# A fused lightning attention and gMLP kernel under another written-out order of its 719 steps

## The chip, the cores and the metric

The kernel runs on one core of one Trainium2 chip. The metric is the device time of one execution in microseconds (us), lower is better. Five engines work side by side, each through its own queue in order: TensorE (PE, the matmuls), VectorE (DVE), ScalarE (ACT), GpSimd (POOL), and SyncE (SP), which here only issues transfers (DMA). An engine that has to wait at one step also holds up every step queued behind it.

## The reference, cut to what matters

Decayed linear attention in blocks of 64 rows over 4 batches, 8 heads, 768 rows and head size 64, followed by a gated MLP whose gate mixes rows with a 768 x 768 matrix:

```python
for b in range(nb):                                   # 12 blocks of 64 rows
    intra = einsum('bhic,bhjc->bhij', qb, kb) * Dmask # lam ** (i - j), lower triangle
    intra = einsum('bhij,bhjd->bhid', intra, vb)
    inter = einsum('bhid,bhde->bhie', qb * lam_pow, kv_state)
    out[:, :, sl] = intra + inter
    kv_state = lam_block * kv_state + einsum('bhsd,bhse->bhde', kb * rev_pow, vb)
x = out.transpose(0, 2, 1, 3).reshape(B, S, H * D)
h = maximum(x @ w_in, 0)                              # 512 -> 1024
u, v = h[..., :512], h[..., 512:]
v_n = (v - mean(v)) / sqrt(var(v) + 1e-06)
v_s = einsum('ts,bsd->btd', w_spatial, v_n) + b_spatial[None, :, None]
y = (u * v_s) @ w_out                                 # 512 -> 512
```

## The kernel before

The decays are powers of one factor per head, so the kernel multiplies the rows of k and q by tables of powers once (`lv`, `lqn`, lines 222 to 227) and then works with a 0/1 mask. All matmul operands are bf16. The work is cut into 12 steps of 256 rows, three to a batch: steps 0 to 2 are batch 0, and so on to steps 9 to 11 for batch 3. Once the three steps of a batch have given their normalised `vn`, the row mixing and the output of that batch can be computed.

The order is fully written out. `ORDER` (line 16) is a string of 719 tokens; `tc.manual_schedule()` (line 610) runs through it, and each token calls one function. Its last letter is the engine: T TensorE, D VectorE, A ScalarE, P GpSimd, S SyncE. The tokens of one letter, read in turn, are that engine's queue. Semaphores are put in where a step reads what another wrote, or overwrites a buffer or PSUM bank that is still read; so an order cannot make a wrong result, but it decides who waits. The numbers behind the name are the step or batch, the part, and the PSUM banks.

| tokens | lines | what they do |
|---|---|---|
| LK, LQ, LV n | 196 | load k, q or v of step n, 512 KB, into one of three buffers (n mod 3), from SyncE |
| lam, BR | 200, 289 | load the 8 factors and the bias row, from ScalarE |
| LB, LN, LL, LX | 216 to 227 | spread the factors, logarithm, the tables of powers |
| msk, idn, posk, one, row | 203 to 240 | mask, identity for the transposes, positions, ones |
| FL k | 309 | k filler matmuls on ones, into a bank that is overwritten later |
| KM, QM n.x | 331 | decayed k or q of half x, f32 to bf16, on VectorE or GpSimd |
| VC, VD n | 185, 181, 183 | v to bf16, whole or in halves |
| TK, TQ; EK, EQ | 366 | transposes on TensorE and their copies out of PSUM (steps 0 to 6) |
| DK, DQ | 344, 348 | the same transposes by DMA, from SyncE (steps 7 to 11) |
| SC, MK | 396, 401 | scores of one half, masked into `a_sb` |
| KP, SY, SX, SA | 425 to 440 | state of the step: matmuls, and the copies and sums of it |
| AV, FN, EX | 468, 459, 481, 487 | attention output, a one-element copy that marks its end, the copy to `xT` |
| WH, CW, CX | 253 to 257 | W_in: four loads, four casts of the v half (CW), two of the u half (CX) |
| WQ, WC, WT, EW | 274 to 563 | W_spatial: six loads, casts, transposes, copies |
| WP, WX | 283 to 286 | W_out: one load of 1 MB, two casts |
| PV, EV, BN | 493, 498, 508 | v = x @ W_in and its relu, row statistics |
| RA, RD, RB, VN | 513 to 532 | 1/sqrt of the variance and the normalised rows `vn` |
| PU, EU | 544, 498 | u, transposed, and its relu |
| GP, PW, GM | 566, 570, 576 | bias put into the bank, the row mixing (6 matmuls) added to it, times u |
| PO, PH; EO, EH; ST, SH | 581 to 604 | output, its copy, its store (256 KB) |
| GN | 536 | a one-element copy on GpSimd that waits for a `vn`, and so holds GpSimd back |

W_in's v half and W_out and two of the W_spatial blocks pass through the same f32 buffer `wst[0]`, so those loads wait for the casts of what lay there. k, q and v have three buffers each, the casts and decays (`kc`, `qc`, `vb`) and the transposed operands (`kT`, `qT`) two.

Of the kernel before, what the change touches and what calls it, by code (L numbers as in the profile page):

```python
# [21 lines left out]
TQ.1.0.1.T FL.4.256.4.1.T TK.1.0.0.T TK.1.1.3.T TQ.1.1.5.T KP.0.2.T AV.0.0.6.4.T QM.2.0.P LK.2.S KM.2.1.P KM.2.0.P
LV.1.S WH.0.S WH.1.S LV.2.S LQ.3.S WH.3.S VD.1.1.P CW.2.P EQ.1.0.1.D SX.0.D EQ.1.1.5.A SY.0.2.A EK.1.1.3.A
FN.0.6.4.D EK.1.0.0.D TQ.2.1.5.T AV.0.1.6.4.T SA.0.1.D EQ.2.1.5.D SC.1.0.1.2.T EX.0.0.6.A EX.0.1.4.A FL.2.256.0.1.T
FL.1.256.3.1.T TQ.2.0.0.T SC.1.1.5.6.T TK.2.1.4.T FL.2.256.3.1.T FL.1.256.3.1.T FL.1.256.3.1.T TK.2.0.3.T
MK.1.0.1.2.D MK.1.1.5.6.D EQ.2.0.0.A VD.1.0.A EK.2.1.4.A KP.1.2.T AV.1.0.0.1.T SY.1.2.D SA.1.0.D FN.1.0.1.D
# [5 lines left out]
EV.2.1.6.A WT.0.0.3.T WT.2.0.5.T EW.2.0.5.A PU.2.1.2.T WT.1.0.0.T BN.2.0.D RD.1.D BN.2.1.D VN.1.1.D RD.0.D RB.0.D
EW.0.0.3.A RA.2.A VN.0.0.A CX.0.P PU.2.0.6.T EU.2.0.6.A VN.0.1.A EW.1.0.0.D RD.2.D LK.3.S PU.1.0.5.T PU.0.0.3.T
VN.2.0.D VN.1.0.D VN.2.1.D LK.4.S WQ.3.S EU.1.0.5.D GP.0.2.0.6.D EU.2.1.2.A GP.0.1.0.5.A EU.0.0.3.A GP.0.3.0.2.A
KM.3.0.P WQ.4.S WQ.5.S LV.3.S LQ.4.S LQ.5.S LV.4.S KM.4.0.P QM.4.0.P QM.4.1.P QM.5.0.P QM.5.1.P VC.4.P PW.0.0.0.1.T
KM.4.1.D KM.3.1.D WC.3.D GM.0.0.0.1.D PW.0.1.0.5.T PW.0.2.0.6.T TK.3.2.0.T WC.4.A EQ.3.2.4.A EK.3.2.0.A WC.5.D
GM.0.1.0.5.D GM.0.2.0.6.D WT.2.1.3.T WT.0.1.1.T EW.0.1.1.D WP.S VC.3.D EW.2.1.3.A GP.0.1.1.6.A PW.0.3.0.2.T
WT.1.1.4.T LK.5.S GM.0.3.0.2.D SC.3.1.0.1.T KP.3.5.T SC.3.0.2.3.T MK.3.1.0.1.D EW.1.1.4.A PW.0.1.1.6.T TK.4.2.0.T
MK.3.0.2.3.D GP.0.3.1.1.A GP.0.2.1.2.A SY.3.5.A PW.0.3.1.1.T SA.3.1.D SX.3.D GM.0.1.1.6.D GP.0.0.1.3.A TQ.4.2.4.T
PW.0.2.1.2.T GM.0.2.1.2.D GM.0.3.1.1.D PW.0.0.1.3.T GM.0.0.1.3.D EK.4.2.0.A EQ.4.2.4.A KM.5.0.P KM.5.1.P  # L40
AV.3.0.5.6.T SC.4.0.1.2.T KP.4.0.T FN.3.5.6.A AV.3.1.5.6.T SY.4.0.D SC.4.1.3.4.T EX.3.1.6.A TQ.5.2.0.T WX.0.A WX.1.A
EX.3.0.5.D MK.4.0.1.2.D SA.4.1.D MK.4.1.3.4.D SA.4.0.D LV.5.S PV.3.1.6.T PU.3.1.5.T PO.0.1.1.T PO.0.3.2.T TK.5.2.4.T
PV.3.0.3.T LV.6.S LK.6.S EK.5.2.4.D EO.0.1.1.A EQ.5.2.0.A EV.3.1.6.A EU.3.1.5.A EO.0.3.2.D VC.5.P AV.4.0.6.0.T
KP.5.6.T SC.5.0.1.2.T EV.3.0.3.A FN.4.6.0.D SC.5.1.4.5.T AV.4.1.6.0.T PU.3.0.3.T VC.6.P SA.5.0.D MK.5.1.4.5.D
MK.5.0.1.2.D KM.6.0.P KM.6.1.P LK.7.S LQ.7.S LQ.6.S KM.7.1.P QM.7.0.P QM.6.0.P QM.6.1.P EX.4.1.0.A EX.4.0.6.A
PV.4.1.0.T PV.4.0.4.T AV.5.0.1.5.T BN.3.1.D FN.5.1.5.D KP.6.2.T AV.5.1.1.5.T EV.4.0.4.A PO.0.2.4.T PO.0.0.6.T
EV.4.1.0.A EX.5.1.5.A EX.5.0.1.A BN.3.0.D PV.5.1.0.T PU.5.1.5.T PV.5.0.1.T KM.7.0.P LV.7.S LV.9.S LQ.8.S LQ.9.S
LK.8.S LV.8.S EO.0.2.4.D EU.3.0.3.A BN.4.1.D RA.3.A RD.3.D GP.1.2.0.4.D GP.1.1.0.3.A SY.6.2.A EV.5.1.0.D
GP.1.0.1.0.A SX.6.A EV.5.0.1.A BN.4.0.D BN.5.1.D BN.5.0.D EO.0.0.6.A RA.4.A PU.4.0.2.T PU.4.1.1.T RD.4.D EU.5.1.5.D
RB.3.D EU.4.0.2.A RA.5.A PO.0.5.6.T PU.5.0.5.T GP.1.1.1.2.A EU.4.1.1.A VN.3.1.A EU.5.0.5.A RD.5.D VN.4.1.D VN.5.0.D  # L50
VN.4.0.D VN.5.1.D EO.0.5.6.D VN.3.0.D SA.6.1.D PO.0.4.1.T TK.6.2.5.T TQ.6.2.6.T EO.0.4.1.A PW.1.1.0.3.T PW.1.1.1.2.T
PW.1.2.0.4.T GM.1.1.1.2.D EQ.6.2.6.D GM.1.1.0.3.D PW.1.0.1.0.T GM.1.2.0.4.D GM.1.0.1.0.D GP.1.3.0.1.A QM.7.1.P
KM.8.0.P KM.8.1.P VC.7.P QM.8.1.P GN.2.1.P QM.8.0.P EK.6.2.5.A GP.1.2.1.0.D GP.1.3.1.2.A DQ.7.S DK.7.S PW.1.3.0.1.T
GM.1.3.0.1.D SC.6.0.5.6.T SC.6.1.3.4.T GP.1.0.0.1.A PW.1.2.1.0.T PW.1.0.0.1.T MK.6.1.3.4.D MK.6.0.5.6.D GM.1.2.1.0.D
GM.1.0.0.1.D PW.1.3.1.2.T GM.1.3.1.2.D AV.6.0.6.0.T FN.6.6.0.A KP.7.3.T SY.7.3.D SC.7.1.4.5.T AV.6.1.6.0.T
SC.7.0.1.2.T EX.6.0.6.A PO.1.4.3.T PO.1.5.6.T QM.9.0.D MK.7.1.4.5.D MK.7.0.1.2.D SA.7.1.D SA.7.0.D EX.6.1.0.A
PV.6.1.4.T EV.6.1.4.D PO.1.0.5.T EO.1.5.6.A VC.8.A EO.1.4.3.A AV.7.0.2.6.T DK.8.S DQ.8.S LK.9.S SC.8.0.0.1.T
FN.7.2.6.A KP.8.6.T SC.8.1.3.4.T AV.7.1.2.6.T EO.1.0.5.A EX.7.0.2.A EX.7.1.6.A MK.8.0.0.1.D SA.8.0.D MK.8.1.3.4.D
BN.6.1.D PV.6.0.5.T PO.1.2.2.T VC.9.A KM.9.1.P KM.9.0.P PV.7.1.6.T EV.7.1.6.D PV.7.0.4.T AV.8.0.0.1.T KP.9.3.T
EV.6.0.5.A GP.2.3.1.6.A EV.7.0.4.A FN.8.0.1.D AV.8.1.0.1.T BN.6.0.D BN.7.0.D EX.8.1.1.A EX.8.0.0.A PU.6.0.5.T  # L60
PU.7.1.4.T GP.2.1.0.1.D SY.9.3.D EU.6.0.5.A EO.1.2.2.D BN.7.1.D EU.7.1.4.A RA.6.A PV.8.1.0.T EV.8.1.0.D PV.8.0.2.T
PU.8.1.3.T PU.6.1.4.T PU.7.0.5.T EV.8.0.2.A EU.8.1.3.A GP.2.2.0.2.A EU.6.1.4.A RA.7.A BN.8.1.D RD.6.D BN.8.0.D
SA.9.1.D RB.6.D VN.6.0.D RD.7.D RA.8.A RD.8.D RB.7.D VN.7.1.A GP.2.0.1.0.A EU.7.0.5.A SX.9.A PO.1.1.3.T PU.8.0.4.T
RB.8.D LQ.10.S LK.10.S ST.0.0.S LV.10.S DK.9.S LQ.11.S VN.7.0.D VN.6.1.D VN.8.0.D VN.8.1.D GP.2.3.0.5.A EU.8.0.4.A
KM.10.0.P QM.9.1.P GN.5.0.P QM.10.0.P QM.10.1.P DQ.10.S LK.11.S ST.0.3.S KM.10.1.P PW.2.3.1.6.T GP.2.2.1.4.D
GM.2.3.1.6.D DQ.9.S KM.11.0.P KM.11.1.P QM.11.0.P QM.11.1.P PW.2.1.0.1.T PW.2.0.1.0.T GP.2.1.1.6.D GM.2.1.0.1.D
GM.2.0.1.0.D PW.2.2.1.4.T PW.2.3.0.5.T ST.0.5.S LV.11.S DK.10.S ST.0.4.S GM.2.3.0.5.D GM.2.2.1.4.D VC.10.A
EO.1.1.3.A GP.2.0.0.3.A PW.2.2.0.2.T GM.2.2.0.2.D SC.9.0.0.1.T SC.9.1.4.5.T PW.2.0.0.3.T PO.1.3.2.T MK.9.0.0.1.D
GM.2.0.0.3.D MK.9.1.4.5.D PW.2.1.1.6.T GM.2.1.1.6.D EO.1.3.2.A KP.10.0.T AV.9.0.1.2.T SY.10.0.D FN.9.1.2.A
SC.10.1.3.4.T SC.10.0.5.6.T AV.9.1.1.2.T EX.9.1.2.A PO.2.0.0.T DK.11.S DQ.11.S ST.1.4.S ST.0.1.S ST.0.2.S EX.9.0.1.D  # L70
PV.9.0.2.T EV.9.0.2.A PV.9.1.1.T MK.10.1.3.4.D MK.10.0.5.6.D EV.9.1.1.A BN.9.1.D SA.10.1.D SA.10.0.D BN.9.0.D
PO.2.3.2.T PU.9.1.3.T VC.11.P EU.9.1.3.A EO.2.0.0.A PO.2.4.5.T EO.2.4.5.A SC.11.1.3.4.T KP.11.6.T SC.11.0.0.1.T
PU.9.0.6.T PO.2.5.5.T MK.11.1.3.4.D RA.9.A RD.9.D MK.11.0.0.1.D SA.11.0.D AV.10.0.3.4.T AV.11.0.0.1.T FN.10.3.4.D
RB.9.D FN.11.0.1.D AV.10.1.3.4.T EO.2.5.5.A AV.11.1.0.1.T EX.11.0.0.A EX.10.0.3.A PO.2.2.5.T EX.10.1.4.D PV.10.1.0.T
PU.10.1.3.T EX.11.1.1.D EV.10.1.0.A EU.10.1.3.A VN.9.0.A PV.10.0.4.T GP.3.1.1.1.D EO.2.2.5.D EO.2.3.2.D BN.10.1.D
EV.10.0.4.A PV.11.1.5.T EV.11.1.5.A EU.9.0.6.D PV.11.0.2.T GP.3.0.1.6.A EV.11.0.2.A BN.10.0.D RA.10.A BN.11.1.D
# [567 lines left out]
```

## Time and profile before

| | |
|---|---|
| median of 3 runs | 145.53 us (145.13 to 146.61) |
| the profiled execution | 144.71 us, of which 143.0 us are its span |
| mean granted TensorE clock | 0.972 |
| busy, TensorE / VectorE / ScalarE / GpSimd | 133.8 / 115.3 / 82.8 / 51.9 us |
| TensorE's share of the chain that ended last | 83% |
| moved by DMA | 33.6 MB, mean 235 GB/s |

The span is what the trace covers; the 1.71 us between it and the time lie around it. The slices of the page cut the span into 40 equal parts of 3.575 us; a digit 9 is 90% busy or more, and PEclk is the granted TensorE clock in tenths of full speed. The chain of waits follows the work that ended last back to the start: each of its pieces is one engine's work, and the next begins where that one released it. Where it stays on one engine, that engine was the limit. The filler matmuls count as TensorE's busy time.

### The profile page before, as it was taken

Reading aid. Unit: us, or ns where it says so; the run is one execution under the profiler, and the core shown is the slowest. Engines: PE = TensorE matmul, PEld = TensorE weight load, DVE = VectorE, ACT = ScalarE, POOL = GpSimd, SP = SyncE. Lnnn points to the kernel's source line nnn. Section 1 sums busy time; section 2 is a strip of 40 time slices with the busy share of each in tenths; the row PEclk is TensorE's granted clock in tenths of the full one; section 3 lists DMA queues with packets and bytes.
Section 4 is the critical chain, followed back from the end, with each engine's and each line's share of the span. In section 5 each row is a group of like instructions: output and inputs, shape, how many; then the busy total and the mean of one; then the engine's idle time right before and its main releaser. Section 6 shows DMA issues by size and latency. Waiting matters only on the chain.

```text
span 143.0 us, 4741 instructions
## 1 busy us (share of the span) xinstructions
PE 133.8 (94%) x1999; PEld 87.7 (61%) x2014; DVE 115.3 (81%) x236; ACT 82.8 (58%) x158; POOL 51.9 (36%) x61
## 2 busy tenths in 40 slices
PE   5969999899999899999999999999999999999990
...
DVE  3399798989997769699399988995798889874760
...
PEclk9975899999999999999999999999999999999998
DMA  3999999899999899959904799998994403930284
GB/s 87 347 347 346 386 323 315 294 339 313 337 302 344 259 288 324 285 166 290 293 0 78 49 282 354 180 142 238 276 257 126 177 5 117 406 139 0 78 324 185
DMA packets 54617, 33.60 MB, mean 235 GB/s; under 512 B 11715, under 2 KB 49859, under 8 KB 54596
## 3 DMA queue, kind: packets, MB, share of 16 engines
...
q8 instruction: 15, 0.25, 0.7%
q10 hardware_dynamic: 148, 0.13, 0.3%
...
## 4 chain that ended last, share of the span: by engine, by line
PE 83%; DVE 9%; ACT 3%; issue 2%; DVEq 0%; ACTq 0%
PE ps L570 21%; PE ps L581 14%; PE ps L493 13%; PE ps L544 11%; PE ps L396 5%; PE ps L366 5%; PE ps L309 4%; PE ps L468 4%; PE ps L425 3%; PE ps L459 2%; DVE st L508 2%; DVE qc L331 2%; DVE kc L331 2%; DVE vn L532 1%; DVE win_sb L183 1%
## 5 line engine op out<-in xcount | busy, mean ns | idle before, releaser
L570 PE MATMUL ps<-wt_sb,vn 128*128 128x384 bf16 x192 | 33.7, 326 | 0.5 <-ACT vn L529 0.3
L331 POOL TENSOR_TENSOR kc<-k_in,lv 128x512 bf16<-128x512 f32 x20 | 20.5, 1043 | 30.0 <-PE ps L493 11.5
L401 DVE TENSOR_TENSOR a_sb<-ps,m 128x1024 bf16<-128x1024 f32 x24 | 28.4, 1211 | 0.7 <-PE ps L425 0.6
L570 PEld LDWEIGHTS <-vn 128*128 128x128 bf16 x192 | 18.3, 98 | 12.3 <-ACT vn L529 0.6
L544 PE MATMUL ps<-xT,win_sb 128*128 128x256 bf16 x192 | 23.6, 273 | 0.5 <-DVE win_sb L183 0.5
L331 POOL TENSOR_TENSOR qc<-q_in,lqn 128x512 bf16<-128x512 f32 x18 | 19.3, 1090 | 10.2 <-DMA q_in<-in_q_dram 5.2
L493 PE MATMUL ps<-win_sb,xT 128*128 128x512 bf16 x89 | 22.3, 379 | 0.4
L581 PE MATMUL ps<-wout_sb,gT 128*128 128x512 bf16 x84 | 22.1, 379 | 0.4
L576 DVE TENSOR_TENSOR gT<-ps,uT 128x384 bf16<-128x384 f32 x32 | 16.8, 551 | 7.1 <-PE ps L570 6.7
L544 PEld LDWEIGHTS <-win_sb 128*128 128x128 bf16 x192 | 18.4, 98 | 5.1 <-DVE win_sb L183 0.7
L181 ACT ACTIVATE ps<-bsp 128x384 f32<-128x384 f32 x23 | 11.2, 490 | 10.7 <-DVE gT L576 6.7
L508 DVE BATCH_NORM_STATS2 st<-vh 128x6 f32<-128x512 bf16 x24 | 16.2, 676 | 1.1 <-ACT vh L498 1.1
L181 ACT ACTIVATE o_sb<-ps 128x512 f32<-128x512 f32 (+1 forms) x14 | 8.0, 579 | 15.4 <-PE ps L581 14.6
L493 PEld LDWEIGHTS <-xT 128*128 128x128 bf16 x96 | 8.8, 98 | 9.6 <-ACT xT L181 0.8
L498 ACT ACTIVATE vh<-ps 128x512 bf16<-128x512 f32 x20 | 11.7, 600 | 4.9 <-PE ps L493 3.2
L181 ACT ACTIVATE xT<-ps 128x512 bf16<-128x512 f32 x20 | 11.0, 598 | 5.8 <-PE ps L468 5.7
L581 PEld LDWEIGHTS <-gT 128*128 128x128 bf16 x92 | 8.7, 98 | 8.6
L498 ACT ACTIVATE uT<-ps 128x512 bf16<-128x512 f32 x20 | 11.7, 590 | 2.0 <-PE ps L544 2.0
L468 PE MATMUL ps<-a_sb,vb 64*64 64x128 bf16 x384 | 10.2, 220 | 0.3 <-issue 0.3
L396 PE MATMUL ps<-qT,kT 64*64 64x128 bf16 x384 | 9.7, 226 | 0.0
L309 PE MATMUL ps<-ones 128*128 128x256 bf16 x32 | 7.5, 368 | 1.6 <-DVE ones L305 1.5
L185 POOL CAST vb<-v_in 128x1024 bf16<-128x1024 f32 (+1 forms) x6 | 5.8, 965 | 7.8 <-PE ps L468 7.8
...
## 6 DMA issues: line engine op xcount, KB each, us to landing
...
```

What stands on the lines that cost most here:

```text
L181: nc.scalar.activation(out=o, in_=i, func=AF.Copy)
L331: vec(e).tensor_tensor(out=dst[n % NCA][:, u].rearrange("p u m o d -> p o (u m) d"), in0=src[n % NIN].rearrange("p (o u) m d -> p o u m d" ...
L396: nc.tensor.matmul(out=pa[o][row(c), w, j], lhsT=kT[n % NTR][row(o), u, j, c * Q64:(c + 1) * Q64], rhs=qv(n, o, u, c), start=(w == 0 and j ...
L401: nc.vector.tensor_tensor(out=a_sb[n % NA][:, i].rearrange("p o w j x -> p o w (j x)"), in0=ps[:, b0:b1 + 1:b1 - b0].rearrange("p o (w y) ...
L468: nc.tensor.matmul(out=po[c ^ o][row(w), c, i], lhsT=vb[n % NCA][row(c), 4 * o + u, j, :], rhs=a[row(c), i, o, w, j, :], start=(r == 0 and ...
L493: nc.tensor.matmul(out=bank(b), lhsT=x[:, slot(c, g)], rhs=win_sb[:, g, DH:DFF], start=(g == 0), stop=(g == NCH - 1))
L498: nc.scalar.activation(out=o, in_=i, func=AF.Relu)
L508: nc.vector.bn_stats(out=st6[p2][:, t], in_=vh[p2][:, t])
L544: nc.tensor.matmul(out=pu[:, f2].rearrange("p (c x) -> p c x", c=2), lhsT=win_sb[:, g, f * P:(f + 1) * P], rhs=x[:, slot(0, g):slot(1, g) ...
L570: nc.tensor.matmul(out=bank(b)[:, 0:HW], lhsT=vn[bb % 2][:, s, f * P:(f + 1) * P], rhs=wt_sb[:, s, i * HW:(i + 1) * HW], start=False, stop ...
L576: nc.vector.tensor_tensor(out=gT[bb % 2][:, f, cols], in0=bank(b)[:, 0:HW], in1=uT[bb % 2][:, f, cols], op=ALU.mult)
L581: nc.tensor.matmul(out=bank(b), lhsT=gT[bb % 2][:, f, t * P:(t + 1) * P], rhs=wout_sb[:, f, :], start=(f == 0), stop=(f == NCH - 1))
```

## The change

Only `ORDER` differs: the same 719 functions are called in another order, on partly other engines and with other PSUM banks; no function is changed. TensorE gets the same 213 tokens, 32 filler matmuls among them. VectorE has 214 tokens instead of 211, ScalarE 152 instead of 160, GpSimd 59 instead of 54, SyncE 81 as before. What moves between engines (tokens before and after):

| | ScalarE | VectorE | GpSimd |
|---|---|---|---|
| decays KM | - | 4, 5 | 20, 19 |
| decays QM | - | 6, 3 | 18, 21 |
| W_in casts CW | 3, 0 | 0, 1 | 1, 3 |
| W_in casts CX | 0, 1 | 1, 0 | 1, 1 |
| v casts VC | 4, 4 | 2, 1 | 5, 6 |
| relus EV and EU | 40, 33 | 8, 15 | - |
| bias GP | 23, 20 | 9, 12 | - |
| vn VN | 7, 9 | 17, 15 | - |
| W_out casts WX | 2, 1 | 0, 1 | - |

The loads, in SyncE's order up to step 5:

```
before: LK.0 LQ.0 LQ.1 LK.1 LV.0 LQ.2 LK.2 LV.1 WH.0 WH.1 LV.2 LQ.3 WH.3 WQ.0 WQ.1 WQ.2 WH.2
        LK.3 LK.4 WQ.3 WQ.4 WQ.5 LV.3 LQ.4 LQ.5 LV.4 WP LK.5 LV.5 LV.6 LK.6 LK.7 LQ.7 LQ.6
after:  LK.0 LQ.0 LV.0 LQ.1 LK.1 LV.1 LK.2 LQ.2 WH.0 WH.1 WH.3 LV.2 WH.2 WQ.1 WQ.0 WQ.2
        LK.3 WQ.3 WQ.5 WQ.4 LQ.3 LV.3 LQ.4 LK.4 LV.4 LQ.5 LK.5 WP LV.5 LK.6 LV.6 LQ.6 LK.9 LQ.7
```

The load of the factors (`lam`) now comes ahead of that of the bias row (`BR`). The diff, cut to its opening and to the other lines that are spoken of below:

```diff
-LK.0.S LQ.0.S LQ.1.S LK.1.S LV.0.S LQ.2.S BR.A lam.A tab.0.A msk.P idn.P posk.P one.D row.D FL.2.256.0.1.T
-FL.2.256.5.1.T FL.2.256.3.1.T FL.2.256.4.1.T FL.2.256.1.1.T FL.1.256.3.1.T FL.2.256.5.1.T LB.1.T LN.1.A eps.D mkc.D
-LL.D LX.A KM.0.0.D QM.0.0.D QM.0.1.D KM.0.1.D FL.1.256.6.1.T BB.1.2.T BB.0.0.T TQ.0.0.3.T FL.2.256.1.1.T TK.0.0.6.T
...
-SC.0.0.2.3.T QM.1.0.P QM.1.1.P KM.1.0.P KM.1.1.P SC.0.1.5.6.T MK.0.0.2.3.D MK.0.1.5.6.D QM.2.1.D FL.2.256.1.1.T
...
-AV.2.1.2.3.T EX.2.0.2.A QM.3.1.D QM.3.0.D TQ.3.2.4.T CX.1.D PU.0.1.0.T PU.1.1.2.T EX.2.1.3.A EV.1.1.6.A BN.0.0.D
...
+lam.A BR.A tab.0.A LK.0.S LQ.0.S LV.0.S LQ.1.S LK.1.S posk.P msk.P row.D one.D FL.2.256.4.1.T FL.2.256.1.1.T
+FL.2.256.0.1.T LB.5.T FL.1.256.0.1.T FL.2.256.3.1.T FL.1.256.4.1.T FL.2.256.2.1.T LN.5.A mkc.D LL.D LX.A KM.0.0.D
+QM.0.0.D QM.0.1.D KM.0.1.P idn.P BB.1.6.T BB.0.5.T TK.0.1.1.T FL.1.256.3.1.T TQ.0.1.3.T TQ.0.0.0.T TK.0.0.4.T
+FL.1.256.2.1.T FL.2.256.2.1.T VC.0.P KP.0.2.T BE.1.6.D EK.0.1.1.A EQ.0.0.0.A EQ.0.1.3.D SY.0.2.A tab.1.A BE.0.5.D
+EK.0.0.4.D QM.1.1.D SC.0.1.0.1.T MK.0.1.0.1.D QM.1.0.P LV.1.S LK.2.S LQ.2.S SC.0.0.4.5.T KM.1.0.P KM.1.1.P
...
+EQ.1.0.1.A EK.1.0.2.A FN.0.0.4.A VD.1.0.P VD.1.1.P KM.2.0.P WH.0.S WH.1.S QM.2.1.P QM.2.0.P SA.0.1.D MK.1.1.5.6.D
...
+TQ.2.0.4.T SA.1.0.D SY.1.3.D EQ.2.0.4.D SC.2.1.5.6.T AV.1.1.1.2.T SC.2.0.3.4.T EX.1.0.1.A EX.1.1.2.A CW.1.P CW.0.P
+CW.2.D MK.2.0.3.4.D MK.2.1.5.6.D SA.1.1.D VC.2.D CW.3.P PV.0.0.0.T PV.1.0.1.T PV.0.1.2.T WH.2.S WQ.1.S WQ.0.S WQ.2.S
...
+GM.0.0.0.5.D PW.0.3.0.0.T GN.2.1.P WT.1.1.2.T WT.2.1.4.T WT.0.1.1.T QM.3.1.P QM.3.0.P GM.0.3.0.0.D EW.0.1.1.D
...
+PW.1.2.0.1.T EU.5.1.0.A EO.0.2.4.A EU.4.1.3.A GM.1.1.1.6.D GP.1.3.1.5.D GP.1.3.0.0.D GP.1.1.0.4.A PW.1.3.1.5.T
+GM.1.2.1.2.D GM.1.2.0.1.D GP.1.0.0.1.A GN.5.0.P QM.7.0.P KM.8.1.D KM.7.0.P KM.8.0.P QM.8.1.P DQ.7.S QM.9.1.P
...
+GM.3.2.0.0.D GP.3.1.0.5.D GP.3.0.0.4.D PW.3.1.0.5.T PH.3.5.0.6.T GM.3.1.0.5.D GM.3.3.0.3.D PW.3.0.0.4.T GM.3.0.0.4.D
```

119 lines of the change are left out of this document (56 added, 63 removed).

## The prediction

> **What bounds the kernel now.** I read the slices first, to see where TensorE is not the limit.
>
> ```profile
> PE   5969999899999899999999999999999999999990
> DVE  3399798989997769699399988995798889874760
> PEclk9975899999999999999999999999999999999998
> DMA  3999999899999899959904799998994403930284
> GB/s 87 347 347 346 386 323 315 294 339 313 337 302 344 259 288 324 285 166 290 293 0 78 49 282 354 180 142 238 276 257 126 177 5 117 406 139 0 78 324 185
> ```
>
> TensorE is full from the tenth slice on (32 us), but for the end. Before that it is patchy, its clock falls to 0.7 and 0.5 in the third and fourth slice, VectorE is as full as TensorE, and DMA moves 294 to 386 GB/s without a pause. So a new order has its room in the first 36 us; later it can mostly lose. Next I read the chain of waits, whose columns are start and length in us.
>
> ```profile
> 6.11 0.69 DVE kc L331
> 6.80 1.20 DVE qc L331 x2
> 8.00 1.48 DVE kc L331
> ...
> 23.96 1.28 DVE qc L331 x2
> 25.24 1.23 DVE win_sb L183
> 26.47 0.61 DVE st L508
> ...
> 31.75 0.30 DVE vn L532
> ...
> 35.81 0.50 ACT ps L181
> 36.36 2.11 PE ps L570 x12
> ...
> 48.12 0.32 issue
> ...
> 49.46 0.13 issue
> ...
> 51.28 1.73 PE ps L581 x8
> ...
> 139.27 0.60 ACT o_sb L181
> ```
>
> Up to 36.36 us the chain runs mainly through VectorE: the decays of step 0, then step 3's q decays and a W_in cast ahead of the row statistics. From there it is TensorE until 139.27. All that TensorE has to do is the same after the change, so I split the forecast into the moment at which the row mixing of batch 0 runs without a break (36.36 us now; called M) and the waits behind M.
>
> **The start.** Last, the timeline: start, length, engine, line, operation, and in brackets the wait before it.
>
> ```profile
> 0.79 0.52 ACTq L289 DMA_DIRECT2D bsp<-in_moe_b_spatial_dram  x1
> 1.34 0.23 ACTq L200 DMA_DIRECT2D lam_in<-in_lam_dram  x1
> 7.88 2.49 POOL L331 TENSOR_TENSOR qc<-q_in,lqn 128x512 bf16<-128x512 f32 x2 [4.96 <-ACT bsp L181]
> 7.92 1.55 DVE L331 TENSOR_TENSOR kc<-k_in,lv 128x512 bf16<-128x512 f32 x1
> 9.26 1.45 SPq L196 DMA_DIRECT2D v_in<-in_v_dram  x1
> 10.80 1.06 ACT L181 ACTIVATE vb<-v_in 128x1024 bf16<-128x1024 f32 x1 [2.93 <-DMA v_in<-in_v_dram]
> 17.28 0.61 POOL L185 CAST vb<-v_in 128x512 bf16<-128x512 f32 x1
> 19.82 2.33 DVE L401 TENSOR_TENSOR a_sb<-ps,m 128x1024 bf16<-128x1024 f32 x2
> ```
>
> And the group of GpSimd's k decays (count, total us, mean ns):
>
> ```profile
> L331 POOL TENSOR_TENSOR kc<-k_in,lv 128x512 bf16<-128x512 f32 x20 | 20.5, 1043 | 30.0 <-PE ps L493 11.5 <-DMA k_in<-in_k_dram 7.9 <-PE ps L366 3.9
> ```
>
> The factors' load goes out at 0.79 instead of 1.34, so tables and first decay come 0.55 us earlier, at 5.56 instead of 6.11. The four decays of step 0 took VectorE to 9.48; now three stay there and one (1.04 us, the mean of the group) goes to GpSimd. They don't run side by side: at 7.92 a VectorE decay stood beside one of GpSimd's and took 1.55 us where the first took 0.69, that is, it waited until GpSimd's was over (7.88 + 1.04 = 8.92) and then ran.
>
> The Trainium skill has this as a rule ("SBUF — State Buffer", section "Who interferes with whom"): VectorE and GpSimd share one pair of ports, and a VectorE instruction with two SBUF inputs, or in a fast copy or cast mode, and a GpSimd instruction that reads SBUF shut each other out until the first is done. The trace agrees (1.55 against 0.69), and the rule speaks against more work on GpSimd.
>
> In turns: 5.56, GpSimd's to 7.2, VectorE's second to 7.85, and the third, behind the mask part of the identity on GpSimd (now after that decay), to about 8.7. That is 0.8 ahead of 9.48, but GpSimd casts v until 9.8 and decays q of step 1 until 10.9, and VectorE's QM.1.1 waits for that, to 11.5. Loads arrive one every 1.45 us (the SyncE row); the fifth landed at 10.80 (ScalarE's cast waited for it). k of step 1 was fourth and is now fifth, 1.5 us later, but GpSimd is not free for it until 11.5 anyway.
>
> From there GpSimd does KM.1.0, KM.1.1, VD twice, KM.2.0, QM.2.1, QM.2.0 and three W_in casts, with VectorE's KM.2.1 in between: 5 x 1.04 + 5 x 0.61 + 0.6 = 8.9 us, to 20.4. VectorE's own W_in cast (CW.2) sits in front of step 2's masks and is shut out until then; masks from 21.25, against 19.82 now: **1.4 us later**. The nearest rows bound this: no collision would give 20.4, one more of 1.04 would give 22.3.
>
> **From the masks to M.** Now VectorE's list from 19.82 to its last `vn`, in the timeline and, for the small line 523, its group.
>
> ```profile
> 29.98 0.69 DVE L508 BATCH_NORM_STATS2 st<-vh 128x6 f32<-128x512 bf16 x1 [0.31 <-ACT vh L498]
> 31.89 1.07 POOL L331 TENSOR_TENSOR kc<-k_in,lv 128x512 bf16<-128x512 f32 x1 [0.99 <-DMA k_in<-in_k_dram]
> 32.16 0.81 DVE L523 SCALAR_TENSOR_TENSOR nmr<-mv,rstd 128x2 f32<-128x2 f32 x1
> 33.54 1.58 DVE L532 TENSOR_SCALAR vn<-vh,mv,rstd 128x512 bf16<-128x512 bf16 x3
> 35.04 0.68 DVE L500 TENSOR_SCALAR uT<-ps 128x512 bf16<-128x512 f32 x1
> ```
>
> ```profile
> L523 DVE SCALAR_TENSOR_TENSOR nmr<-mv,rstd 128x2 f32<-128x2 f32 x8 | 1.8, 232 | 0.0
> ```
>
> It ends at 35.04, after 15.2 us. Out of it go step 3's q decays (1.28), the W_in cast (1.23, now on ScalarE), 0.67 of the 0.81 at 32.16 (its seven others took (1.8 - 0.81) / 7 = 0.14; GpSimd was busy until 31.89 + 1.07 = 32.96), and another 0.65 in the three `vn` (1.58 against 3 times the 0.30 of the chain's first): GpSimd now stands still behind GN.2.1 until the last `vn`. Also 0.3 of waiting ahead of 29.98. Into it come a relu of v and one of u (0.68 each, by the row at 35.04), a W_spatial cast and a bias copy (0.55 each, as the 0.50 of ScalarE's bias copy), and one more `vn` (0.30). That is -4.1 + 2.8 = -1.3; from 21.25, 13.9 us lead to 35.15. ScalarE's bias copy, on which M hung (35.81 + 0.50), is queued early enough now; M becomes 35.55, **-0.8 us**. With the bounds above: 34.7 to 36.6.
>
> **Behind M.** VectorE gets 15 relus for 8, 3 more bias copies, one of the W_out casts and both `xT` copies of step 3, against 3 q decays fewer, 2 `vn` fewer and smaller ones: about +3.6 us in all, 2 of it between M and batch 1's row mixing, where TensorE has some 32 us to do. So the slack gets thin, and I price four places.
> - WC.4 and WC.5 on VectorE meet QM.3.1 on GpSimd, which GN.2.1 lets go at the same moment: one waits 1.04. VectorE's queue hands it to step 3's transposes (bank 5, read by GM.0.0); 0.4 is slack: +0.65.
> - Both `xT` copies of step 3 stand behind two products GM: TensorE waits 0.6 at PV.3.0, where it now loses 0.32 + 0.13 at 48.12 and 49.46: +0.15.
> - TK.5 waits for EV.3.0 on VectorE (bank 5): +0.25.
> - KM.7.1 and KM.8.1 on VectorE between the products of batch 1 (at most 1.04 of shut-out, mostly under mixings of 1.05 us, 2.11 for two at 36.36), step 9's v cast behind QM.10.1, and at the end a bias copy on VectorE ahead of the eighth mixing: +0.15, +0.2, +0.15.
>
> W_out later costs nothing: its load is the 28th of SyncE's; with it 14.4 MB are loaded, which the first 13 slices moved (4080 GB/s x 3.575 us = 14.6 MB, 46.5 us), so it and its casts are there by 49 us. The first output now starts at 51.28 and later after the change, behind more of the products of batch 0, which hide it; without that cover each us of lateness is a us of time. k of step 9 ahead of k of steps 8 and 7 waits for KM.6.1 and holds SyncE a few us, but step 7 is wanted only at about 68. The end is as now: last output, 0.6 of ScalarE's copy, one store.
>
> **Sum**: -0.8 + 0.65 + 0.15 + 0.25 + 0.5 = +0.75. The profiled execution took 144.71 (span 143.0 + 1.71 around it) and would take 145.5; it lies 0.8 below the median, 145.53, to which I add: **146.3 us**.
>
> **The rivals.**
> - *The gain at the start holds and nothing is given back* (chance 0.31). The factors' load could land earlier still, since nothing stands ahead of it; then step 0's decays begin when k lands and miss the collisions: masks at 20.4, M at 34.7, -1.65. The waits of 0.45 near 49 us go, as step 3's loads come in time and GpSimd has the decays. 145.53 - 2.1 = 143.4 us. For it: 36 us of patchy TensorE. Against: VectorE is as full as TensorE there, and isn't relieved.
> - *The shut-out decides* (0.25). GpSimd gets five more steps, so more of VectorE's casts, decays and `vn` meet one. Five places could hand a full 1.04 to TensorE: QM.1.1, CW.2, WC.5, the W_out cast, KM.8.1. All would be 5.2, less 0.8 already counted: +4.4, 150.7 us. I take three: +2.3, 148.6 us. It decides from the second collision behind M that finds TensorE's next bank not free. For it: 0.81 us for a row of 0.14, and VectorE's digits of 9 and 8 between M and 60 us. Against: TensorE often has other products queued.
> - *The clock* (0.08). It is at 0.7 and 0.5 in slices 3 and 4. GpSimd makes the identity only after its first decay, so TensorE idles near 8 us; if half clock lasts three us more, matmuls that fill them take 1.5 longer: 147.8 us.
> - That the change does nothing measurable is within the forecast's own spread (0.36), 144.4 to 148.1.
>
> **How the numbers follow.** About 1%, 1.46 us, is what a measurement here can tell from no change. Faster: 0.27 of the first rival and 0.02 of the forecast, 0.29. Within 1%: 0.26 of the forecast, 0.04 and 0.02 of the first and third, 0.32. Slower: 0.25 + 0.08 of the forecast + 0.06 of the clock, 0.39. The cases of both signs hold most of the chance. The range reaches from just under the first rival, 142.8, to 149.4, past most of the second, whose top of 150.7 stays outside; about 0.15 is left out.
>
> **What would show it.** First decay at 5.6 us; step 2's masks near 21 us; an unbroken row of mixings from about 35.5; a VectorE cast of some 1.5 us there; waits of TensorE near 39 and 48 us; no wait on W_out. Wrong is the forecast if M is before 34.7 or past 36.6, or if TensorE's waits behind M, its end apart, add up to over 2 us more than now.

## The result, and the profile after

| | median | runs | ratio to the kernel before |
|---|---|---|---|
| before | 144.80 us | 20 | |
| changed | 146.10 us | 20 | 1.0109 [1.0084, 1.0133] |

The changed kernel is 1.1% slower: 0.0109 x 144.8 = 1.6 us (1.2 to 1.9). The ratios, here and below, come from the fast runs alone (those within 1.5% of the same kernel's fastest), so they are not the quotients of the medians (1.0090 here). The prediction was 146.3 us. The profiled execution of the changed kernel took 145.34 us, 143.6 of it its span; that of the kernel before 144.71 and 143.0.

The slices of the changed kernel's page:

```profile
PE   5999998999999999899979999999999989999990
...
PEclk9999999999999999999999999999999999999997
```

TensorE's row is nearly full from the second slice on, where it was patchy up to the tenth. (The 9s of PEclk in the first slices don't show a full clock; the last section says why.) In exchange there is a 7 in the 21st slice (20 x 3.59 = 71.8 to 75.4 us), where there was none. So the start got better, and something behind it worse. Where, the chains of waits say. First the kernel before, from batch 1 on (start, length in us):

```profile
74.87 1.24 PE ps L570 x7
...
97.17 5.85 PE ps L570 x36
...
126.25 3.90 PE ps L570 x24
```

And the changed kernel:

```profile
33.62 2.93 PE ps L570 x18
...
72.25 1.68 DVE kc L331
...
74.45 0.42 PE ps L396 x16
74.86 1.25 PE ps L570 x7
...
98.06 4.88 PE ps L570 x30
...
103.51 3.03 PE ps L570 x18
...
126.86 5.85 PE ps L570 x36
...
139.89 0.60 ACT o_sb L181
```

The last twelve mixings of batch 0 began at 36.36 before. Now all 18 run in one go from 33.62, so the last twelve begin at 33.62 + 6 x 2.93 / 18 = 34.60: **M is 1.76 us earlier**. It is no mere shift of work: the 65 TensorE tokens ahead of the first mixing are the same in both orders, but for one transposition of step 3 (TK.3.2 in place of TQ.3.2, 8 matmuls each). The scores of step 6 (line 396) begin at 73.12, and began at 74.23, so 0.65 of the gain is lost ahead of them. The next mixing behind them comes at 74.86 against 74.87: the whole gain is gone by then, and the new links are VectorE's, above all one k decay of 1.68 us. The mixings of batch 2 stand 0.03 later once the output that now lies ahead of them is counted: 98.06 - 0.86 = 97.20 against 97.17 (0.86 is what four matmuls of line 581 take in the chain). Those of batch 3 are at +0.61, the last output copy at +0.62 (139.27 before). So there is something to explain up to 75 us, above all near 72, and something between 97 and 126. The timeline shows both. The first, with one row of the kernel before and then the changed kernel:

```profile
74.23 0.64 PE L396 MATMUL ps<-qT,kT 64*64 64x128 bf16 x32
```

```profile
65.42 1.02 ACT L181 ACTIVATE qT<-ps 128x1024 bf16<-128x1024 bf16 x1 [0.22 <-PE ps L366]
66.75 0.42 DVE L440 TENSOR_TENSOR s_sb<-ps,ysb 128x256 bf16<-128x256 f32 x1 [0.37 <-ACT s_sb L181]
...
68.33 0.40 DVE L532 TENSOR_SCALAR vn<-vh,mv,rstd 128x512 bf16<-128x512 bf16 x1
...
68.79 4.40 PE L570 MATMUL ps<-wt_sb,vn 128*128 128x384 bf16 x26 [0.15 <-DVE vn L532]
...
72.17 1.76 DVE L331 TENSOR_TENSOR kc<-k_in,lv 128x512 bf16<-128x512 f32 x1
72.34 3.48 POOL L331 TENSOR_TENSOR qc<-q_in,lqn 128x512 bf16<-128x512 f32 x3
73.12 0.42 PE L396 MATMUL ps<-qT,kT 64*64 64x128 bf16 x16
...
74.45 0.42 PE L396 MATMUL ps<-qT,kT 64*64 64x128 bf16 x16 [0.91 <-DVE gT L576]
```

The decay at 72.17 is KM.8.1. A VectorE decay takes 0.69 alone; this one began while GpSimd was at a k decay (until 72.37), with three q decays right behind, and took 1.76. The product `gT` behind it (GM.1.3.1.5) frees the bank that half of step 6's scores go into, and TensorE waited 0.91 for it. Earlier, VectorE waited 0.37 for the state copy SX.6 of ScalarE, which stood behind the 1.02 us copy EQ.6; the last `vn` of batch 1 stands behind that wait. The second place:

```profile
115.11 0.14 DVE L183 COPY seen<-ps 1x1 f32<-1x1 f32 x1
115.28 0.16 ACT L181 ACTIVATE seen<-ps 1x1 f32<-1x1 f32 x1 [1.00 <-DVE seen L183]
115.49 0.31 PE L459 MATMUL ps<-qT,s_sb 64*64 64x128 bf16 x8 [0.52 <-ACT seen L181]
```

FN.10, a one-element copy on ScalarE that TensorE waits for, was itself waiting for FN.11 on VectorE, which writes the same element; and FN.11 stood behind a bias copy and the state sum of step 11. In the kernel before, FN.10 was on VectorE itself, ahead of FN.11.

### The profile page after: what moved, and what is told of

Its sections match the earlier page's. It is cut to its first block, busy times and chain, and to the rows that moved or that the text cites. A ratio compares the mean times of both kernels' runs of the same rounds, so it can differ in the third digit from the quotient of the medians.

```text
span 143.6 us, 4757 instructions
## 1 busy us (share of the span) xinstructions
PE 135.5 (94%) x2014; PEld 87.6 (61%) x2014; DVE 118.7 (83%) x239; ACT 78.8 (55%) x150; POOL 58.3 (41%) x66
## 4 chain that ended last, share of the span: by engine, by line
PE 86%; DVE 7%; issue 3%; ACT 1%; DVEq 0%
PE ps L570 19%; PE ps L493 14%; PE ps L581 14%; PE ps L544 13%; PE ps L366 6%; PE ps L396 5%; PE ps L468 4%; PE ps L309 4%; PE ps L459 2%; PE ps L425 2%; PE ps L295 2%; DVE kc L331 2%; PE ps L556 1%; DVE ps L183 1%; DVE a_sb L401 1%
## 5 line engine op out<-in xcount | busy, mean ns | idle before, releaser
L331 POOL TENSOR_TENSOR qc<-q_in,lqn 128x512 bf16<-128x512 f32 x21 | 22.0, 1058 | 14.7 <-DMA q_in<-in_q_dram 12.3
L493 PE MATMUL ps<-win_sb,xT 128*128 128x512 bf16 x96 | 23.5, 379 | 0.0
L581 PE MATMUL ps<-wout_sb,gT 128*128 128x512 bf16 x92 | 22.6, 379 | 0.0
L181 ACT ACTIVATE ps<-bsp 128x384 f32<-128x384 f32 x20 | 9.7, 491 | 9.2 <-DVE gT L576 7.7
L181 ACT ACTIVATE o_sb<-ps 128x512 f32<-128x512 f32 (+1 forms) x13 | 7.3, 581 | 13.1 <-PE ps L581 7.2
L498 ACT ACTIVATE vh<-ps 128x512 bf16<-128x512 f32 x17 | 9.9, 593 | 6.8 <-PE ps L493 5.1
L498 ACT ACTIVATE uT<-ps 128x512 bf16<-128x512 f32 x16 | 9.4, 591 | 3.5 <-PE ps L544 3.4
L185 POOL CAST vb<-v_in 128x1024 bf16<-128x1024 f32 (+1 forms) x8 | 7.7, 967 | 4.3 <-DMA v_in<-in_v_dram 4.2
L181 ACT ACTIVATE kT<-ps 128x512 bf16<-128x512 bf16 (+1 forms) x8 | 6.1, 757 | 5.3 <-PE ps L366 5.3
```

What stands on the lines that cost most here:

```text
L181: nc.scalar.activation(out=o, in_=i, func=AF.Copy)
L331: vec(e).tensor_tensor(out=dst[n % NCA][:, u].rearrange("p u m o d -> p o (u m) d"), in0=src[n % NIN].rearrange("p (o u) m d -> p o u m d" ...
L493: nc.tensor.matmul(out=bank(b), lhsT=x[:, slot(c, g)], rhs=win_sb[:, g, DH:DFF], start=(g == 0), stop=(g == NCH - 1))
L498: nc.scalar.activation(out=o, in_=i, func=AF.Relu)
L581: nc.tensor.matmul(out=bank(b), lhsT=gT[bb % 2][:, f, t * P:(t + 1) * P], rhs=wout_sb[:, f, :], start=(f == 0), stop=(f == NCH - 1))
```

## The experiments

Each is timed against the kernel before on the same chip, 6 to 12 runs each, in three sets on three chips. The last column compares with the changed kernel: the ratio divided by 1.0109, the half-widths of the two intervals combined by their squares, times 146.1 us. The changed kernel was not timed again beside them, so the whole column shares that one figure: with the medians' 1.0090 in its place, every entry would be about 0.3 us higher, that is, each gain smaller. What an edit gives is therefore also read from its trace, over the short stretch that it touches.

| kernel | median, us | ratio to before | against the changed kernel, us |
|---|---|---|---|
| KM.8.1 on GpSimd | 144.58 | 1.0011 [0.9979, 1.0043] | -1.4 +- 0.6 |
| KM.8.1 two products later | 145.39 | 1.0040 [1.0005, 1.0075] | -1.0 +- 0.6 |
| FN.10 ahead, on ScalarE | 145.92 | 1.0102 [1.0057, 1.0147] | -0.1 +- 0.7 |
| FN.10 ahead, on VectorE | 144.90 | 1.0046 [1.0015, 1.0077] | -0.9 +- 0.6 |
| SX.6 ahead of EQ.6 | 145.36 | 1.0046 [1.0009, 1.0084] | -0.9 +- 0.7 |
| all three mended | 143.49 | 0.9906 [0.9870, 0.9942] | -2.9 +- 0.6 |
| bias row's load first | 146.12 | 1.0096 [1.0056, 1.0137] | -0.2 +- 0.7 |
| W_in cast CX.1 on VectorE | 145.69 | 1.0105 [1.0048, 1.0162] | -0.1 +- 0.9 |
| q decays of step 3 on VectorE | 147.07 | 1.0183 [1.0121, 1.0245] | +1.1 +- 1.0 |
| *before*, q decays of step 3 on GpSimd | 144.56 | 0.9981 [0.9945, 1.0018] | |
| *before*, KM.8.1 on VectorE | 145.43 | 1.0065 [1.0024, 1.0107] | |
| *before*, the same a product earlier | 146.24 | 1.0146 [1.0089, 1.0202] | |

### KM.8.1 back on GpSimd

```diff
-GN.5.0.P QM.7.0.P KM.8.1.D KM.7.0.P KM.8.0.P QM.8.1.P DQ.7.S
+GN.5.0.P QM.7.0.P KM.7.0.P KM.8.0.P KM.8.1.P QM.8.1.P DQ.7.S
```

> The changed kernel with one step moved: the second half of step 8's k decay (KM.8.1) back from VectorE to GpSimd, behind KM.8.0. Theory 1 (the shut-out at this one place): in the changed kernel KM.8.1 took 1.76 us instead of 0.68 and kept the product GM.1.3.1.5 from freeing the bank that the scores SC.6.1 need, and TensorE stood still 0.91 us there; without it SC.6.1 follows SC.6.0 at once and the time falls by 0.9 to 1.3 us. Rival (VectorE is simply full): the 0.68 us of work leave, the waits move to the masks of step 6, and the time falls by 0.3 us or less. Rival (the DMA transposes of steps 7 and 8 set the pace there): no change.

It took 1.4 us off, nearly all of what the change had lost. Its chain at that place:

```profile
68.19 4.40 PE ps L570 x26
72.58 0.57 PE ps L396 x32
73.16 3.03 PE ps L570 x18
```

The mixings and all of the scores of step 6 run without a break, and the next mixing starts at 73.16 instead of 74.86. Not all of this is the edit's: the 26 mixings ahead of it, which it doesn't touch, already start 0.60 earlier (68.19 against 68.79). From there to the mixing behind the scores it takes 4.97 us instead of 6.07, so the decay cost **1.10 us at its place**. This stretch hardly varies: in five other kernels of the changed order with the decay where it was, it is 6.07 or 6.08. The last output copy is 1.19 earlier (138.70 against 139.89).

### KM.8.1 on VectorE, two products later

```diff
-QM.7.0.P KM.8.1.D KM.7.0.P
+QM.7.0.P KM.7.0.P
...
-GM.1.3.0.0.D SC.6.0.2.3.T
+GM.1.3.0.0.D KM.8.1.D SC.6.0.2.3.T
```

> The changed kernel with KM.8.1 still on VectorE, but two steps later, behind the products GM.1.3.1.5 and GM.1.3.0.0. Theory 1 (the place decides): SC.6.1 no longer waits for it; the masks of step 6 come up to 1.8 us later instead, of which three row mixings (2.9 us) cover part; the time falls by 0.3 to 0.7 us, less than with the decay on GpSimd. Rival (VectorE is simply full): no change, since the same work stays on the same engine.

VectorE keeps the work, and the place alone gives 1.0 us. In its profile (147.59 us, late by some 2 us from 65 on) the decay still takes 1.26 beside GpSimd's, at 75.64, but both halves of the scores run in one go, and what is left is a wait of 0.32 for a mask behind the decay. So it was not VectorE's load that cost most, but what stood behind this step.

### FN.10, first on ScalarE, then on VectorE

```diff
-AV.10.0.1.2.T EU.9.1.0.A PV.9.0.0.T
+AV.10.0.1.2.T FN.10.1.2.A EU.9.1.0.A PV.9.0.0.T
...
-FN.11.6.4.D EV.9.0.0.A FN.10.1.2.A AV.10.1.1.2.T
+FN.11.6.4.D EV.9.0.0.A AV.10.1.1.2.T
```

> The changed kernel with the one-element copy FN.10 (ScalarE) put ahead of FN.11 (VectorE) in the written order, right behind AV.10.0. Theory: both write the same one-element buffer, so FN.10 had to wait for FN.11, which stood behind a bias copy and a state sum on VectorE, and AV.10.1 on TensorE waited 0.52 us for FN.10. With the new order TensorE runs AV.10.1 right behind AV.11.0 and the time falls by 0.4 to 0.6 us. Rival: the wait moves to AV.11.1, which needs FN.11 anyway, and no more than 0.2 us is gained.

No gain: the last output copy is at 140.06, against 139.89. Neither the theory nor its rival had the reason, which the timeline shows:

```profile
112.64 0.16 ACT L181 ACTIVATE seen<-ps 1x1 f32<-1x1 f32 x1 [1.50 <-PE ps L468]
112.70 0.57 ACT L498 ACTIVATE uT<-ps 128x512 bf16<-128x512 f32 x1
113.33 1.02 PE L493 MATMUL ps<-win_sb,xT 128*128 128x512 bf16 x3 [0.80 <-ACT uT L498]
```

FN.10 now waited 1.50 us for its attention output with a relu queued behind it, and TensorE waited 0.80 for that relu. The wait had only moved. The second attempt puts it on the engine of FN.11, ahead of it, with the bias copy behind both:

```diff
-GP.3.3.1.5.D SA.11.0.D FN.11.6.4.D EV.9.0.0.A FN.10.1.2.A
+SA.11.0.D FN.10.1.2.D FN.11.6.4.D GP.3.3.1.5.D EV.9.0.0.A
```

> The changed kernel with the acknowledgement FN.10 on VectorE ahead of FN.11, and the bias copy GP.3.3.1.5 behind both; no other edit. Theory (the wait of 0.52 at 115.49 was FN.10 behind FN.11 through the shared tile, and moving it on ScalarE only held up the relu behind it): the wait goes and nothing takes its place, last output 0.4 to 0.6 earlier, time 0.3 to 0.6 us shorter than the changed kernel's. Rival (this place has no slack, another wait follows): the last output moves by less than 0.2, the time is the same.

```profile
114.53 0.14 DVE L183 COPY seen<-ps 1x1 f32<-1x1 f32 x1
...
115.03 0.14 DVE L183 COPY seen<-ps 1x1 f32<-1x1 f32 x1 [0.37 <-PE ps L468]
...
115.23 0.31 PE L459 MATMUL ps<-qT,s_sb 64*64 64x128 bf16 x8
```

Both acknowledgements come in time, no wait stands at TensorE's matmul, and the time falls by 0.9 us. The last output copy is 0.60 earlier (139.29). From the last 18 mixings of batch 2 to those of batch 3 it takes 22.76 us (103.51 to 126.27) instead of 23.35, so this place is worth **0.59**; with FN.10 ahead on ScalarE it took 23.68.

### SX.6 ahead of EQ.6

```diff
-RD.4.D EQ.6.2.0.A PU.4.1.3.T PO.0.0.5.T SX.6.A
+RD.4.D SX.6.A EQ.6.2.0.A PU.4.1.3.T PO.0.0.5.T
```

> The changed kernel with one ScalarE copy moved: the state copy of step 6 (SX.6) ahead of the 1.02 us copy of step 6's q transposition, instead of behind it. In the changed kernel's trace VectorE waited 0.37 for this copy at 66.75 and its last normalised tile of batch 1 began at 68.33. Theory (that wait sets the start of batch 1's mixings): the tile comes 0.3 to 0.5 earlier, the row of mixings runs without the small break, end of the scores of step 6 0.3 to 0.4 earlier, time 0.2 to 0.5 us shorter than the changed kernel's. Rival (the mixings wait for the lock of KM.8.1 alone): it comes earlier and waits longer there, time the same within 0.2.

Its chain:

```profile
71.93 1.68 DVE kc L331
...
74.55 3.03 PE ps L570 x18
```

The long decay is still there, 0.32 earlier (72.25), and so is the row of batch 3, by 0.31 (126.55 against 126.86). These starts alone don't show a gain: in three kernels of the changed order that leave SX.6 where it was, the same timeline row begins at 71.57, 71.79 and 71.81, earlier than here (71.85). But from the `vn` ahead of the wait (66.06 here, 65.90 in the changed kernel) to the mixing behind step 6's scores it takes 8.49 us instead of 8.96, and 8.97 or 8.96 in those three: **0.47** at this place. The rival doesn't hold; TensorE's wait for KM.8.1 got shorter, from 0.91 to 0.76. The timed gain of 0.9 +- 0.7 is consistent with that and no better resolved.

### All three together

The edits are those of KM.8.1 on GpSimd, SX.6 ahead of EQ.6 and FN.10 on VectorE, as above.

> The changed kernel with three steps moved: KM.8.1 on GpSimd behind KM.8.0 (as in the first of these runs), SX.6 ahead of the q copy of step 6, and at the start of batch 3's last steps the acknowledgement FN.10 on VectorE ahead of FN.11 (it stood on ScalarE behind it), with the bias copy GP.3.3.1.5 behind both. If the three losses add up (1.2 to 1.6 for KM.8.1 as timed, 0.3 for SX.6, 0.5 at 115.49), it takes 1.9 to 2.4 us less than the changed kernel, 143.6 to 144.1 beside a changed kernel at 146.1. Rival (each wait taken away is followed by the next one, as moving FN.10 on ScalarE gave nothing): as the kernel with KM.8.1 alone, 144.4 to 144.8, the same as before.

```profile
72.61 0.57 PE ps L396 x32
...
124.59 5.85 PE ps L570 x36
...
137.61 0.60 ACT o_sb L181
```

The three single gains, 1.4 + 0.9 + 0.9, come to 3.2; together they give 2.9, above the 1.9 to 2.4 expected, with the interval reaching down to 2.3. By their stretches, 1.10 + 0.47 + 0.59 = 2.16. The last output copy is 2.28 earlier than in the changed kernel, where it had lost 2.38 since M (1.76 + 0.62), and 1.66 earlier than in the kernel before. So these three places are nearly all of the loss. With a ratio of 0.9906 [0.9870, 0.9942] this kernel beats both.

### Where the gain at the start came from

Three reversals on the changed kernel, one at a time. First the order of the two small loads:

```diff
-lam.A BR.A tab.0.A
+BR.A lam.A tab.0.A
```

> The changed kernel with the two loads of ScalarE's queue swapped back: the bias row goes out ahead of the decay factors, as in the kernel before. Theory (M is 1.76 us earlier because the factors land 1.3 us earlier when they are issued first, and the decays of step 0 start when k lands): first decay at 5.6 to 6.2 instead of 4.86, batch 0's unbroken row of mixings 0.7 to 1.3 us later than in the changed kernel's trace, time 0.3 to 1.3 us longer. Rival (the gain came from what left VectorE between the masks and M; the first decay has slack, as VectorE waits for q at 6.28 anyway): M moves by less than 0.4 and the time by less than 0.3.

Then a W_in cast, from ScalarE to VectorE behind step 2's masks:

```diff
-CX.0.P CX.1.A WQ.3.S
+CX.0.P WQ.3.S
...
-MK.2.1.5.6.D SA.1.1.D
+MK.2.1.5.6.D CX.1.D SA.1.1.D
```

> The changed kernel with one W_in cast (CX.1, 1.06 us on ScalarE) put back on VectorE, right behind the masks of step 2. Theory V (VectorE's list between those masks and the last normalised tile sets the start of the row mixings of batch 0, as the prediction had it): the list is 1.23 longer, the unbroken row of mixings begins 1.0 to 1.3 later than in the changed kernel's trace, where x18 began at 33.62, and the time is 0.7 to 1.3 us longer. Theory T (TensorE, busy 13.3 of 14 us from 20 to 34 us, sets it, and VectorE has slack): the row begins 0 to 0.6 later, as it came only 0.49 later when the masks came 1.31 later, and the time is at most 0.5 us longer.

Then the q decays of step 3, from GpSimd to VectorE ahead of the row statistics, with their load ahead:

```diff
-LV.2.S MK.1.0.1.2.D
+LV.2.S LQ.3.S MK.1.0.1.2.D
...
-SA.2.0.D BN.0.0.D
+SA.2.0.D QM.3.1.D QM.3.0.D BN.0.0.D
```

> The changed kernel with the q decays of step 3 (QM.3.1, QM.3.0) back on VectorE ahead of the row statistics of batch 0, as in the kernel before, and q's load of step 3 issued behind v of step 2, so that it is there in time. Theory V: the list is 1.28 to 1.4 longer and the unbroken row of mixings begins 1.0 to 1.5 later; time 0.7 to 1.4 us longer. Theory T: the row begins 0 to 0.6 later and the time is at most 0.5 us longer. The earlier load puts 512 KB ahead of the W_in loads, which by itself can cost up to 1.45, one row of SyncE's; then the W_in casts, not VectorE, are late.

Their chains at the mixings of batch 0, in this order (three kernels):

```profile
34.11 2.92 PE ps L570 x18
```

```profile
33.89 2.93 PE ps L570 x18
```

```profile
25.62 1.71 DVE qc L331 x2
...
34.92 3.00 PE ps L570 x16
```

By the last twelve, M is 35.08, 34.87 and 34.92 + 4 x 3.00 / 16 = 35.67. The measure has a spread: in the changed kernel and five others with the same order up to there, the row of 18 began at 33.61, 33.62, 33.62, 33.88, 33.89 and 34.15, so M lies between 34.59 and 35.12. For the order before there are two more profiles with the same start (the two below with KM.8.1 on VectorE): M 36.12 and 36.49. So the gain at M is 1.0 to 1.9, clear of the spread. Two of the three reversals are inside the changed order's spread. The load of the factors moved the first decay by 0.67 (5.53 against 4.86), but neither M nor the time beyond the spread; step 2's masks, at 20.74, are hardly later than the 20.53 of one kernel with the changed order's start. The cast took 0.68 on VectorE, not the 1.31 that the same cast took before (at 25.16, beside one of GpSimd's), so its list got only that much longer, and TensorE had the slack. Only the q decays, 1.71 us for the two at 25.62, moved M clearly, and the time by 1.1 +- 1.0. There the chain from the masks (20.82) to the mixings is VectorE's own list, as the prediction had it. Masks as late as that (20.53, 20.74) went with M at 35.12 and 35.08, so about 0.55 of it is the decays'; how much their load did to the masks, the run doesn't part.

The other way round, the same decays put on GpSimd in the kernel before:

```diff
-VD.1.1.P CW.2.P EQ.1.0.1.D
+VD.1.1.P CW.2.P QM.3.1.P QM.3.0.P EQ.1.0.1.D
...
-EX.2.0.2.A QM.3.1.D QM.3.0.D TQ.3.2.4.T
+EX.2.0.2.A TQ.3.2.4.T
```

> The kernel before with one part of the change alone: step 3's two q decays (QM.3.1, QM.3.0) from VectorE to GpSimd, behind its W_in cast CW.2, where GpSimd stands still. Theory 2 (the gain of the start is VectorE's relief ahead of the row statistics): 1.28 us leave VectorE's chain at 23.96, the row mixing of batch 0 begins 0.8 to 1.3 us earlier than 36.36, and as nothing later is changed, the time falls by as much. Rival (a start that is ahead is given back, because the loads of batch 1 set the pace behind it): the mixing begins earlier, but the time falls by less than 0.4 us. Rival (the shut-out): GpSimd's decays lengthen VectorE's casts at 22 us, and the mixing does not begin earlier.

In its profile 17 mixings run from 34.65 on, which puts M at 34.65 + 5 x 2.98 / 17 = 35.53, 0.6 to 1.0 ahead of the order before, and the last copy comes 1.02 earlier (138.25); the time fell by 0.3 +- 0.5 us only. So moving these decays is a part of the gain at M, 0.55 to 1.0 by the two runs; that the time follows is not shown, and the rest of the gain at M has no run of its own.

### The suspected cost, put into the kernel before

```diff
-EQ.6.2.6.D GM.1.1.0.3.D PW.1.0.1.0.T
+EQ.6.2.6.D GM.1.1.0.3.D KM.8.1.D PW.1.0.1.0.T
...
-KM.8.0.P KM.8.1.P VC.7.P
+KM.8.0.P VC.7.P
```

> The kernel before with one step moved the other way: the k decay KM.8.1 from GpSimd to VectorE, between two products GM of batch 1, where GpSimd decays q and k at the same time. Theory (a VectorE decay beside GpSimd's takes 1.5 to 1.8 us instead of 0.68, and the products behind it hold TensorE up): one decay of 1.3 to 1.8 on VectorE near 72 to 74 us, a wait of TensorE of 0.4 to 1.2 for a product GM behind it, time 0.4 to 1.3 us longer than before. Rival (TensorE has other products queued here, three mixings ahead of the scores of step 6): the long decay shows, but TensorE loses less than 0.3 and the time is the same.

The profiled execution shows no long decay:

```profile
71.45 1.03 POOL L331 TENSOR_TENSOR qc<-q_in,lqn 128x512 bf16<-128x512 f32 x1
...
72.47 0.68 DVE L331 TENSOR_TENSOR kc<-k_in,lv 128x512 bf16<-128x512 f32 x1
...
74.73 2.44 PE L570 MATMUL ps<-wt_sb,vn 128*128 128x384 bf16 x14 [0.41 <-DVE ps L183]
```

GpSimd's was over at 72.48, a hundredth of a us after VectorE's began. Span and last output are as before, but the time is 0.9 +- 0.6 us longer. The place has a cost even so: TensorE waits 0.41 for a bias copy of VectorE that now stands behind the decay, and from the start of batch 1's mixings to the end of the 18 behind the scores it takes 9.11 us (68.71 to 77.82) instead of 8.64 (69.26 to 77.90), 0.47 more. So 0.68 us of work at this place costs something without any lock. For the lock the step went one product ahead, into the middle of GpSimd's decay:

```diff
-GM.1.1.1.2.D EQ.6.2.6.D
+GM.1.1.1.2.D KM.8.1.D EQ.6.2.6.D
```

> The kernel before with KM.8.1 on VectorE one product earlier than in the last run of this kind, so that it starts near 71.5 us, when GpSimd has just begun a q decay (71.45 to 72.48 there). Theory: it takes 1.6 to 1.7 us instead of 0.68, the products GM behind it come about a us later, TensorE waits 0.4 to 1.2 for one of them, and the time is 0.4 to 1.3 us longer than before. Rival (three mixings and the scores of step 6 are queued ahead of the first product that TensorE needs): the long decay shows, but TensorE loses less than 0.3.

```profile
71.34 1.63 DVE L331 TENSOR_TENSOR kc<-k_in,lv 128x512 bf16<-128x512 f32 x1
71.39 1.03 POOL L331 TENSOR_TENSOR qc<-q_in,lqn 128x512 bf16<-128x512 f32 x1
...
75.62 3.09 PE L570 MATMUL ps<-wt_sb,vn 128*128 128x384 bf16 x18 [0.65 <-DVE ps L183]
```

Now the decay takes 1.63, TensorE waits 0.65 and, between the scores, another 0.22; the last output copy is 1.00 later (140.27) and the time 2.1 +- 0.8 us longer. The same stretch takes 10.06 us (68.65 to 78.71), 1.42 more than before and 0.95 more than in the last run, which met no lock. So the cost, and the lock's part in it, show in an order that has nothing else of the change. The last copy hides some of it, as batch 1's mixings began 0.5 to 0.6 earlier in these two profiles than in that of the kernel before; by the stretch, 0.47 and 1.42 lie inside the timed intervals.

## Why the prediction was right, and where not

The forecast of "slightly slower" came true, but as the sum of a gain that was twice as large as written (1.76 against 0.8) and losses that were half as large again (2.38 against 1.55 by the last output copy), and the losses stood in other places than the priced ones. That 146.3 met 146.1 so closely is partly luck: it was built on a median of 145.53 from 3 runs, which is 144.80 from 20, and what it added was 0.75, where the change cost 1.6.

- **The first decay.** Predicted 5.56, it began at 4.86: the factors, issued with nothing ahead of them, were there by 3.04, and then k's landing set the start. The prediction had carried over the old time from issue to use.
- **The shut-out at step 0.** It was there, but the other way round. The changed kernel's timeline:

```profile
4.86 0.69 DVE L331 TENSOR_TENSOR kc<-k_in,lv 128x512 bf16<-128x512 f32 x1 [0.78 <-DMA k_in<-in_k_dram]
4.91 1.55 POOL L331 TENSOR_TENSOR kc<-k_in,lv 128x512 bf16<-128x512 f32 x1 [2.45 <-DMA k_in<-in_k_dram]
6.28 1.42 DVE L331 TENSOR_TENSOR qc<-q_in,lqn 128x512 bf16<-128x512 f32 x2 [0.72 <-DMA q_in<-in_q_dram]
```

  GpSimd's decay took 1.55, as it waited for VectorE's 0.69, and VectorE's next decays waited for q, not for GpSimd.
- **Step 2's masks.** Predicted 21.25, 1.4 later; they came at 19.43, 0.4 earlier. This term failed: it let VectorE's cast CW.2 wait for the whole of GpSimd's queue. That queue did end at 19.99, near the 20.4 written, but the cast went in between GpSimd's own and took 0.43:

```profile
17.83 2.16 POOL L185 CAST win_sb<-wst 128x512 bf16<-128x512 f32 x3 [0.30 <-DMA wst<-in_moe_w_in_dram]
```

```profile
19.09 0.43 DVE L183 CAST win_sb<-wst 128x512 bf16<-128x512 f32 x1 [0.31 <-DMA wst<-in_moe_w_in_dram]
19.43 2.35 DVE L401 TENSOR_TENSOR a_sb<-ps,m 128x1024 bf16<-128x1024 f32 x2
```

- **From the masks to M.** The prediction let a late mask come through in full. It doesn't: masks at 20.74 and 20.53 (bias row first; all three mended) gave M 35.08 and 35.12, where masks at 19.43 gave 34.60. From 20.04 us to the mixings the changed kernel's chain is TensorE's own work but for 0.64 us, not VectorE's list. The 0.4 that the prediction put between the end of the list and M (35.15 to 35.55) came without a row; in the changed kernel it is 0.54 (34.06 to 34.60). So M at -1.76, or -1.0 to -1.9 over the spread, against -0.8. At 34.60 it is just ahead of 34.7, so by the prediction's own sign the forecast was wrong there.
- **The four places behind M**, 1.55 us in all. WC.4 and WC.5 against QM.3: nothing, because GN.2.1 met them instead (it took 0.91, at 34.13) and QM.3 came behind, at 35.01. The copies of step 3 and TK.5: nothing; TensorE is busy for 21.99 of the 22 us from 34 to 56, so the waits named for 39 and 48 us did not come. Of the fourth, 0.5 for several steps, one alone was worth 1.10 at its place and 1.4 by the times: KM.8.1. The prediction named this step and its lock, and put most of it "under mixings"; what stood behind it was the one product whose bank the scores needed. This is the term that was mis-sized most.
- **What had no price at all**: SX.6 behind EQ.6 and FN.10 behind FN.11, 0.47 and 0.59 at their places, 0.9 each by the times. Both are tokens of a few tenths of a us in ScalarE's queue: EQ.6 came from VectorE and was put ahead of SX.6, and FN.10 came from VectorE, where it had stood ahead of FN.11. Behind M the prediction had priced steps of VectorE and GpSimd, and none of ScalarE.
- **W_out later** cost almost nothing, as written: the first output starts at 51.08 (51.28 before) without a wait, and its eight matmuls took 1.86 instead of 1.73.
- **The rivals.** "The shut-out decides" had the right mechanism with one collision instead of three, and its counter-argument, that TensorE has other products queued, failed at that one place. "The gain holds" had the start right (the first decay waits for k's landing, M near 34.7) and is what the kernel with all three mended shows: 0.94% faster than the kernel before, 1.4 us, where the rival had 2.1; that its 143.4 meets the 143.49 measured is again the old median. The clock's rival did not come: the half rate ended earlier than before, as the last section shows.

By the Trainium skill's rule for VectorE and GpSimd ("SBUF — State Buffer", "Who interferes with whom") a decay on one that meets a decay on the other has to wait until that one is over. The traces agree, with 1.76 and 1.63 us for VectorE decays that take 0.68 alone, and 1.55 for one of GpSimd's that takes 1.04 alone. What a lock costs the kernel is another matter: moving KM.8.1 away from it gave 1.10 us at the place where the scores' bank hung on it, and the lock at step 0 has no run of its own.
